# Casting v without DVE, loads held back by one-element writes, and longer planned DMA latencies in a fused attention and feed-forward kernel

## The chip, the cores and the metric

The kernel runs on one core of one Trainium2 chip. Its time is the device time of one execution in microseconds; "the time" of a kernel is the median of its runs. A profile is taken of one further execution.

The engines are named as the profile names them: PE (TensorE, matmuls), PEld (its weight loads, which overlap the matmuls), DVE (VectorE), ACT (ScalarE), POOL (GpSimd) and SP (SyncE, which only issues DMAs here). SPq and POOLq are the sequencers of SP and POOL.

## The reference

Attention with normalized q and k over 8 batches of 12 heads (448 positions, 64 wide), followed by a feed-forward layer of 3584 rows:

```python
def rmsnorm(x, g):
    rms = np.sqrt(np.mean(x * x, axis=-1, keepdims=True) + 1e-06)
    return x / rms * g
q_n, k_n = (rmsnorm(q, g_q), rmsnorm(k, g_k))
scores = scale * np.matmul(q_n, k_n.transpose(0, 1, 3, 2))
attn = np.exp(scores - np.max(scores, axis=-1, keepdims=True))
attn = attn / (np.sum(attn, axis=-1, keepdims=True) + 1e-09)
x = np.matmul(attn, v)          # heads side by side: (3584, 768)
h = x @ w_in                    # (3584, 2048)
g = h * np.clip(h + 3.0, 0.0, 6.0) / 6.0
out = g @ w_out                 # (3584, 768)
```

## The kernel before, in words

Heads are taken two at a time: 48 pairs, six to a batch. Each pair goes through these steps, whose lines are those that the profile shows:

- **Load.** k, q and v of a pair come in by DMA into slots of the staging tiles `qk_st` (k at index 0, q at index 1) and `v_st`, eight slots each (`NS`). From pair 4 on, the first 384 positions of two pairs come with one DMA (`load_main`, L325), and the last 64 of four pairs with one DMA for q (`load_rest`, L331) and two for k and for v (L333). All of these are issued on SP's queue. A load may overwrite its slot once the pair eight before has been read.
- **Norm.** Squares (`square`, L356 on POOL or DVE, L354 on ACT), sums over 64 (`sums`, L359, DVE), the reciprocal root (`rstd`, L365 and L366, ACT), and the product in bfloat16 (`normalize`, L369, POOL or DVE), which writes `qkn`. For the first eight pairs (`NFAST`) the squares and normalizations come in halves that several engines may take; later they are POOL's.
- **Transposes.** Eight PE transposes (L385) into PSUM, then copies to `qkT` (L397, L399, L336). From pair 20 on a DMA transpose on SP's queue (L390) takes their place.
- **Scores and weights.** Score matmuls (L408), the exponential on ACT (L418), and the weighted sum with v (`weigh`, L431), whose stationary operand is the exponentials and whose moving operand is `vaug`. `vaug` is v of the pair in bfloat16 with a column of ones, one of four buffers (`NV`); it is filled by `cast_v`, L336. So the cast for pair p waits until pair p - 4 has been weighed.
- **Division and x.** DVE divides (L439, L440); `xn` is transposed by PE and copied by DVE into `xT` (L450, L461), or from pair 18 on by a DMA transpose (L454).
- **Feed-forward.** Once six pairs of a batch are in `xT`, the first matrix (L464, `h_mm`), the gate on ACT and DVE (L470, L475), then the second matrix (L483, `y_mm`), the copy to `y_sb` (L336) and the store (L494, L496) on SP's queue. The weights come by DMAs on POOL's queue (L348), which cast to bfloat16 on the way.

The order of every engine's instructions is written by a planner in Python (`Plan`) when the program is built. It keeps a clock for each engine, a price for each operation on each engine that may do it (`ways`), and a model of the DMA queues: `ISSUE` is the time of an issue, `DEPART` the time until a transfer starts to flow, `LAND` the time from its end until the data may be used, and `size` the time for which it occupies the queue. At each step it begins, on each free engine, the ready operation with the least key. Engines are in-order: what the planner puts first runs first, and every instruction waits for what it really depends on, by semaphores. A dependency that only the planner is told of does not become a wait on the chip.

`slot_free` is such a list of dependencies for a load: the normalizations (for v the casts) of the pairs that were in the slots before, and from pair 8 on also the normalizations of the pair `LA` = 4 back. The first part is a true dependency on the tile. The second is only the planner's: the chip does not wait for it.

Of the kernel before, what the change touches and what calls it, by code (L numbers as in the profile page):

```python
# [44 lines left out]
class Plan:  # L45
# [1 line left out]

    HOP = 60
    PRICE, FIRST, UNTIL = {"POOL": 0.5, "ACT": 2.0, "DVE": 1.5}, {"POOL": 0.7, "ACT": 1.5, "DVE": 0.9}, 45e3
    ISSUE, DEPART, LAND, BULK, DEPTH = 620, 1000, 1100, 0.64, 8  # L50
    STEADY, SLACK, LATE = 60e3, 500, {"load": 3500, "turn": 2000}
    LAG = {"POOL": 45, "ACT": 105, "DVE": 85}
    UNITS = 4
# [9 lines left out]
    def add(self, key, ways, deps=(), lag=0, size=0, hold=False, want=None, cell=None):  # L63
        op = Op(key, ways, deps, lag, size, want, cell)
        op.left += hold
        op.subs = 0
        self.todo += 1
        if op.left == 0:
            self.known.append(op)
        return op  # L70
# [155 lines left out]
def kernel(  # L226
# [11 lines left out]
    nc = tc.nc  # L238
# [13 lines left out]
    NS = 8  # L252
# [19 lines left out]
    qk_st = const.tile([P, 2, NS, 2, 4, D], FP32, name="qk_st")  # L272
# [27 lines left out]
    plan = Plan(share=(1.3, 1.0, 0.45, 3.0, 0.4))  # L300
    add = plan.add
# [9 lines left out]
    def blocks(src):  # L311
        return src[:, 0:FULL, :].rearrange("h (p t) d -> p h (t d)", t=NT)

    def halves_of(src):
        return [src[h::2, FULL:S, :].rearrange("h p d -> p h d") for h in range(2)]

    def stage(a, p, n):

        r = slice(p % NS, p % NS + n)
        return heads((k, q, v)[a], p, n), v_st[:, r] if a == 2 else qk_st[:, a, r]  # L320

    def load_main(eng, a, p, n):
        src, st = stage(a, p, n)
        dst = st.rearrange("p r h t d -> p (r h) t d")
        eng.dma_start(out=dst[:, :, 0:NT, :].rearrange("p h t d -> p h (t d)"), in_=blocks(src))  # L325

    def load_rest(eng, a, p, n, half):
        src, st = stage(a, p, n)
        if a == 1:
            dst = st.rearrange("p r h t d -> p (r h) t d")[lo, :, NT, :]  # L330
            eng.dma_start(out=dst, in_=src[:, FULL:S, :].rearrange("h p d -> p h d"))  # L331
        else:
            eng.dma_start(out=st[(lo, hi)[half], :, half, NT, :], in_=halves_of(src)[half])  # L333

    def copy(eng, out, in_):
        (eng.copy if eng is nc.scalar else eng.tensor_copy)(out=out, in_=in_)  # L336
# [38 lines left out]
    def cast_v(eng, p):  # L375
        copy(
            eng, out=vaug[p % NV][:, :, :, 0:D].rearrange("p t h d -> p h t d"),
            in_=v_st[:, p % NS],
        )
# [140 lines left out]
    def load_g(eng):  # L520
        for dst, src in ((gq_t, g_q), (gk_t, g_k)):
            eng.dma_start(out=dst[lo, :], in_=src.rearrange("(p o) -> p o", o=1))
# [7 lines left out]
    V, G, A_ = nc.vector, nc.gpsimd, nc.scalar  # L530
# [4 lines left out]
    def at(xs, i):  # L535
        return xs[i] if 0 <= i < len(xs) else None
# [5 lines left out]
    nrm, vc, tr, pq, pk, wgh, div, xo, px = ([] for _ in range(9))  # L542
# [78 lines left out]
    W_AFTER, LA, VL = 2, 4, 1.2  # L621
# [16 lines left out]
    kb = 780  # L638
    landed, squares, norms = ({}, {}, {}), [], {}

    def slot_free(a, p, n, ahead):

        old = [x for i in range(p, p + n) for x in ([vc[i - NS]] if a == 2 else norms[i - NS]) if i >= NS] \
            if p >= NS else []
        return old + norms.get(p - ahead, []) * (p >= 8)

    def load(a, p, main, rest, rank, aq=nc.sync, qq="SP"):
        if main:
            op = plan.dma((p + rank, a), 1, main * 580, lambda: load_main(aq, a, p, main), slot_free(a, p, main, LA), queue=qq)
            for i in range(p, p + main):  # L650
                landed[a].setdefault(i, []).append(op)
        if rest:
            for half in range(1 if a == 1 else 2):
                op = plan.dma((p + rank, a + 0.1), 1, rest * (200 if a == 1 else 100),
                              lambda half=half: load_rest(aq, a, p, rest, half), slot_free(a, p, rest, LA), queue=qq)
                for i in range(p, p + rest):
                    landed[a].setdefault(i, []).append(op)
        return op

    lg = mg = None  # L660
    for p in range(NPAIR):
        if p == 0:
            lg = plan.dma((-3, 0), 2, 10, lambda: load_g(nc.gpsimd), queue="POOL", issue=900)
            for a, aq, qq in ((0, nc.sync, "SP"), (1, nc.scalar, "ACT")):
                load(a, 0, 1, 1, 0, aq, qq)
            load(0, 1, 1, 0, 0)
            load(1, 1, 1, 0, 0, nc.scalar, "ACT")
            load(0, 1, 0, 3, 0.2)
            load(1, 1, 0, 3, 0.2)
            add((1, 1.5), [("ACT", 1300, lambda: nc.scalar.preload_act_table_set("natural_log_exp_and_others"))])  # L670
            mg = add((-1, 0), [("DVE", 300, make_g)], [lg])
            load(0, 2, 2, 0, 0)
            load(1, 2, 2, 0, 0)
            load(2, 0, 2, 4, V0)
            lv = load(2, 2, 2, 0, V2)
            for w in w_ops:
                lv.next.append(w)
        elif p in REST_OF or p in MAIN_OF:
            for a in range(3):
                load(a, p, MAIN_OF.get(p, 0), REST_OF.get(p, 0), VL if a == 2 else 0)  # L680

# [28 lines left out]
        for a in range(2):  # L710
            ways = [("POOL", 1000, lambda p=p, a=a: normalize(G, p, a)), ("DVE", 1200, lambda p=p, a=a: normalize(V, p, a))]
            norms[p].append(add((p - 2, 4), ways[:2 if p < NFAST else 1], [s2[a], at(tr, p - NQ)]))
        vc.append(add((p, 5), [("DVE", 700, lambda p=p: cast_v(V, p)),
                               ("POOL", 575, lambda p=p: cast_v(G, p)),
                               ("ACT", 530, lambda p=p: cast_v(A_, p))],
                      [*landed[2][p], at(clo, p), at(clv, p // 2), weighed.get(p - NV)]))

        old = scored.get(p - NK, [])
# [4 lines left out]
        else:  # L723
            cell = {}
# [101 lines left out]
```

## Time and profile before

| what | us |
|---|---|
| time, median of 3 runs (lowest to highest) | 446.86 (446.25 to 447.33) |
| the profiled execution's own time | 448.29 |
| its span | 446.5 |
| DVE busy | 243.0 |
| ACT busy | 259.6 |
| POOL busy | 211.1 |
| DMA queue of SP, share of 16 engines' span | 51.0% |
| DMA queue of POOL, share | 10.2% |

The span is from the first to the last instruction of the profiled execution, and its own time has what lies around it. In the lists of groups a row has the line, the engine, the operation, the tile written and read, shapes and the number of instructions; then the busy time and the mean of one. In the timeline a row has its start, its length, and in brackets how long the engine sat idle before it and what ended that. In a table of stretches the busy times of PE, PEld, DVE, ACT and POOL follow the length, each with the number of instructions, and then the granted clock of PE as a share of full speed, the DMA share and GB/s. Rows for a tile or a line give the least, median and greatest duration in nanoseconds.

### The profile page before, as it was taken

To read this page: it belongs to the slowest core of one execution; us is meant where nothing else is said; L and a number is where in the kernel's file an instruction comes from. 1 tells how busy PE (TensorE), PEld (TensorE's weight loads), DVE (VectorE), ACT (ScalarE), POOL (GpSimd) and SP (SyncE) were. 2 spreads that over 40 slices of the span, in tenths; PEclk is the share of its full clock that TensorE was granted. 3 is DMA by queue.
4 is the path that set the end of the run, shared out by engine and by line. 5 is a ranking of instruction groups with operands and counts; after the bars stand their busy time and mean duration, and the time that the engine had idled before them with its cause. 6 is when DMAs were issued, how large, how long until landed. Compare 5 with 4: busy or idle time off the path is not lost.

```text
span 446.5 us, 9002 instructions
## 1 busy us (share of the span) xinstructions
PE 415.3 (93%) x3576; PEld 235.9 (53%) x3576; DVE 243.0 (54%) x421; ACT 259.6 (58%) x478; POOL 211.1 (47%) x204
## 2 busy tenths in 40 slices
PE   0878499999999999999999999999999999999995
PEld 0445265545655555555455655555556555555563
DVE  6899698866864466445546355333435243343321
ACT  3979278987567687777767577676652032132100
POOL 5999569988886676667637554401100000000000
PEclk9989599999999999999999999999999999999999
DMA  7999909999838999886885775243212301100021
GB/s 198 261 255 245 245 0 201 241 258 209 193 94 189 213 193 218 155 215 151 187 202 139 182 164 136 47 95 84 72 24 60 84 1 52 56 37 35 37 72 71
DMA packets 118011, 62.21 MB, mean 139 GB/s; under 512 B 67280, under 2 KB 114384, under 8 KB 117968
## 3 DMA queue, kind: packets, MB, share of 16 engines
q1 hardware_dynamic: 106784, 54.90, 51.0%
q0 software_dynamic: 10496, 6.29, 10.2%
q8 instruction: 28, 0.46, 0.5%
q10 hardware_dynamic: 688, 0.43, 0.3%
q14 instruction: 15, 0.12, 0.1%
HBM read 45.61 MB, written 11.01 MB: 127 GB/s over the span
## 4 chain that ended last, share of the span: by engine, by line
PE 69%; POOL 10%; DVE 7%; DMA 7%; issue 3%; SPq 2%; ACT 1%; POOLq 0%; DVEq 0%; ACTq 0%
PE ps L483 25%; PE ps L464 23%; PE av L431 6%; PE sc L408 6%; PE sc L483 5%; POOL qkn L369 5%; DMA qk_st<-in_q_dram 5%; POOL sq L356 4%; DVE ssq L359 2%; DVE vaug L336 2%; PE sc L464 2%; DMA qkT<-qkn 1%; DVE gT L475 1%; SPq L333 1%; DMA gk_t<-in_g_k_dram 1%
## 5 line engine op out<-in xcount | busy, mean ns | idle before, releaser
L464 PE MATMUL ps<-xT,w_in_sb 128*128 128x448 bf16 x732 | 169.2, 355 | 7.9 <-DVE xT L461 5.9
L418 ACT ACTIVATE eD<-sc 128x896 bf16<-128x896 f32 x144 | 127.3, 915 | 31.7 <-PE sc L408 25.6
L483 PE MATMUL ps<-w_out_sb,gT 128*128 128x384 bf16 x752 | 141.4, 326 | 1.2 <-DVE gT L475 1.1
L470 ACT ACTIVATE t_sb<-ps 128x448 f32<-128x448 f32 x122 | 66.3, 543 | 91.1 <-PE ps L464 87.9
L475 DVE SCALAR_TENSOR_TENSOR gT<-t_sb,ps 128x448 bf16<-128x448 f32 x122 | 75.4, 618 | 72.3 <-ACT t_sb L470 72.0
L483 PEld LDWEIGHTS <-gT 128*128 128x128 bf16 x896 | 82.0, 98 | 60.9 <-issue 12.9
L369 POOL TENSOR_TENSOR qkn<-qk_st,rstd 128x512 bf16<-128x512 f32 x90 | 93.6, 1059 | 26.9 <-ACT rstd L366 16.8
L464 PEld LDWEIGHTS <-w_in_sb 128*128 128x128 bf16 x768 | 68.7, 98 | 63.9 <-issue 18.4
L356 POOL TENSOR_TENSOR sq<-qk_st 128x1024 f32<-128x1024 f32 (+1 forms) x49 | 85.8, 1761 | 7.2 <-DMA qk_st<-in_q_dram 5.7
L431 PEld LDWEIGHTS <-eD 128*128 128x128 bf16 x1152 | 53.6, 99 | 22.6 <-issue 4.5
L359 DVE TENSOR_REDUCE ssq<-sq 128x16 f32<-128x1024 f32 (+1 forms) x50 | 58.3, 1169 | 12.0 <-POOL sq L356 11.2
L408 PE MATMUL sc<-qkT 64*128 64x448 bf16 (+1 forms) x336 | 60.4, 364 | 3.2 <-ACT qkT L336 1.2
L336 DVE COPY y_sb<-ps 128x384 f32<-128x384 f32 x42 | 23.4, 557 | 72.2 <-PE ps L483 72.2
L431 PE MATMUL av<-vaug,eD 128*128 128x65 bf16 x1152 | 59.9, 195 | 0.0
L336 POOL CAST vaug<-v_st 128x512 bf16<-128x512 f32 x34 | 20.8, 618 | 77.6 <-PE av L431 77.6
L440 DVE TENSOR_TENSOR xn<-av,rden 128x512 bf16<-128x512 f32 x48 | 33.2, 692 | 1.7
L418 ACT ACTIVATE eR<-sc 128x448 bf16<-128x448 f32 x48 | 25.9, 539 | 11.4 <-PE sc L408 11.2
L408 PEld LDWEIGHTS <-qkT 64*128 64x128 bf16 (+1 forms) x336 | 14.4, 95 | 30.2 <-issue 24.8
L483 PE MATMUL sc<-w_out_sb,gT 128*128 128x384 bf16 x144 | 25.5, 326 | 0.0
L385 PE MATMUL ps<-identity,qkn 128*128 128x128 bf16 x120 | 11.0, 237 | 13.7 <-POOL qkn L369 11.5
L385 PEld LDWEIGHTS <-qkn 128*128 128x128 bf16 x160 | 11.1, 106 | 17.0 <-POOL qkn L369 11.9
L431 PE MATMUL av<-vaug,eR 128*128 128x130 bf16 x192 | 19.2, 224 | 0.0
(51 smaller groups left out, 178.2 us busy)
## 6 DMA issues: line engine op xcount, KB each, us to landing
v_st<-in_v_dram SPq DMA_DIRECT2D x24, 384.0 KB, 5.8
out_dram<-y_sb SPq DMA_DIRECT2D x24, 384.0 KB, 2.8
qk_st<-in_k_dram SPq DMA_DIRECT2D x23, 384.0 KB, 6.0
qk_st<-in_q_dram SPq DMA_DIRECT2D x23, 384.0 KB, 5.2
w_in_sb<-in_moe_w_in_dram POOLq DMA_DIRECT2D x8, 384.0 KB, 7.3
w_out_sb<-in_moe_w_out_dram POOLq DMA_DIRECT2D x4, 768.0 KB, 11.0
v_st<-in_v_dram SPq DMA_DIRECT2D x24, 64.0 KB, 4.9
out_dram<-y_sb SPq DMA_DIRECT2D x8, 192.0 KB, 2.9
```

The costliest lines, as they stand in the source:

```text
L336: (eng.copy if eng is nc.scalar else eng.tensor_copy)(out=out, in_=in_)
L356: eng.tensor_tensor(out=sq, in0=x, in1=x, op=A_MULT)
L359: nc.vector.tensor_reduce(out=ssq_r[p % NR][:, a].rearrange("p a s -> p (a s)"), in_=sq_r[m % 2][:, a].rearrange("p a s d -> p (a s) d"), ...
L369: eng.tensor_tensor(out=qkn_r[p % NQ][:, a].rearrange("p t h d -> p h t d"), in0=qk_st[:, a, p % NS], in1=rstd_r[p % NR][:, a].rearrange(" ...
L408: nc.tensor.matmul(out=bank(u, h)[:, 0:S], lhsT=qkT[rows, 0, i * P:(i + 1) * P], rhs=qkT[rows, 1, 0:S], start=True, stop=True,)
L418: nc.scalar.activation(out=e[..., 0:S], in_=src[..., 0:S], func=EXP, bias=0.0, scale=1.0)
L431: nc.tensor.matmul(out=out, lhsT=e_tile(p, i, h)[:, c0:c0 + P], rhs=rhs, start=first and j % 2 == 0 and h == 0, stop=last, skip_group_chec ...
L440: nc.vector.tensor_tensor(out=xn_r[p % NQ][:].rearrange("p n (h d) -> p n h d", h=2), in0=av4[:, :, :, 0:D], in1=rden[:].unsqueeze(3).to_b ...
L464: nc.tensor.matmul(out=bank(m)[:, 0:S], lhsT=w_in_sb[:, kt, f * P:(f + 1) * P], rhs=xT[:, kt, b % NX, x_slot(b)], start=(kt == 0), stop=(k ...
L470: nc.scalar.activation(out=t[:], in_=bank(m)[:, 0:S], func=RELU, bias=0.5, scale=1.0 / 6.0,)
L475: nc.vector.scalar_tensor_tensor(out=gT[:, f, (b % 2) * S:(b % 2 + 1) * S], in0=t[:], scalar=1.0, in1=bank(m)[:, 0:S], op0=A_MIN, op1=A_MULT,)
L483: nc.tensor.matmul(out=bank(m)[:, 0:n], lhsT=gT[:, f, c0:c0 + P], rhs=w_out_sb[:, f, c:c + n], start=(f == 0), stop=(f == NFT - 1),)
```

## The change

Three things change, all in the program's text for the planner, with one new kind of instruction:

1. `cast_v` may be done by POOL or ACT, no longer by DVE.
2. For each even pair from 8 to 46, POOL writes one element of zero into k's slot of that pair (`hold`), placed in the plan after the normalizations of the pairs four and eight back. The loads of that pair depend on it in the plan; the load of k that covers the element also does on the chip, since both write the same place. `slot_free` no longer has the planner's own dependency.
3. The planner's numbers: `ISSUE` 630 (620), `DEPART` 1300 (1000), `LAND` 1400 (1100), and the size of the rest loads 150 and 75 for each pair (200 and 100).

```diff
-    ISSUE, DEPART, LAND, BULK, DEPTH = 620, 1000, 1100, 0.64, 8
+    ISSUE, DEPART, LAND, BULK, DEPTH = 630, 1300, 1400, 0.64, 8
...
-    def slot_free(a, p, n, ahead):
+    def slot_free(a, p, n):
 
         old = [x for i in range(p, p + n) for x in ([vc[i - NS]] if a == 2 else norms[i - NS]) if i >= NS] \
             if p >= NS else []
-        return old + norms.get(p - ahead, []) * (p >= 8)
+        return old
+
+    held = {}
+
+    def hold(p):
+
+        cell = qk_st[0:1, 0, p % NS, 0, 0, 0:1]
+        held[p] = [add((-5, p), [("POOL", 80, lambda: nc.gpsimd.memset(cell, 0.0))], norms[p - LA] + norms[p - NS])]
 
     def load(a, p, main, rest, rank, aq=nc.sync, qq="SP"):
         if main:
-            op = plan.dma((p + rank, a), 1, main * 580, lambda: load_main(aq, a, p, main), slot_free(a, p, main, LA), queue=qq)
+            op = plan.dma((p + rank, a), 1, main * 580, lambda: load_main(aq, a, p, main), slot_free(a, p, main) + held.get(p, []), queue=qq)
...
-                op = plan.dma((p + rank, a + 0.1), 1, rest * (200 if a == 1 else 100),
-                              lambda half=half: load_rest(aq, a, p, rest, half), slot_free(a, p, rest, LA), queue=qq)
+                op = plan.dma((p + rank, a + 0.1), 1, rest * (150 if a == 1 else 75),
+                              lambda half=half: load_rest(aq, a, p, rest, half), slot_free(a, p, rest) + held.get(p, []), queue=qq)
...
         elif p in REST_OF or p in MAIN_OF:
+            if p >= NS:
+                hold(p)
             for a in range(3):
                 load(a, p, MAIN_OF.get(p, 0), REST_OF.get(p, 0), VL if a == 2 else 0)
...
-        vc.append(add((p, 5), [("DVE", 700, lambda p=p: cast_v(V, p)),
-                               ("POOL", 575, lambda p=p: cast_v(G, p)),
+        vc.append(add((p, 5), [("POOL", 575, lambda p=p: cast_v(G, p)),
                                ("ACT", 530, lambda p=p: cast_v(A_, p))],
                       [*landed[2][p], at(clo, p), at(clv, p // 2), weighed.get(p - NV)]))
```

The built program issues, on POOL, 35 casts of v (34 before), 89 normalizations (90), 7 half squares (9) and the 20 one-element writes; on ACT 13 casts (11), 8 half squares (6) and 11 copies of y (5); on DVE no cast (3), 7 normalizations (6), 45 copies of y (51). SP issues the same DMAs, in the same order until its 69th.

## The prediction

> **What bounds the kernel now.** I read the page's busy times first, then the table of stretches, then PE's waits, then the timeline around the longest of them.
>
> ```profile
> span 446.5 us, 9002 instructions
> PE 415.3 (93%) x3576; PEld 235.9 (53%) x3576; DVE 243.0 (54%) x421; ACT 259.6 (58%) x478; POOL 211.1 (47%) x204
> PEclk9989599999999999999999999999999999999999
> ```
>
> TensorE is busy for 415.3 of 446.5 us, so the end moves only with PE's 31.2 idle us or with the clock at which it works. The clock line (tenths of full speed, 40 slices of 11.2 us) has one deep dip, in the fifth slice (44.7 to 55.8 us), and a slight one in the third. PE's waits, in the view that names who let it go:
>
> ```profile
> PE ps L385 <- POOL qkn L369: 11.5, 3, 10.6
> PE ps L464 <- DVE xT L461: 5.9, 1, 5.9
> PE ps L385 <- DVE qkn L369: 2.1, 2, 1.8
> PE ps L464 <- DVE gT L475: 1.5, 2, 0.9
> ```
>
> The columns are total, times and longest. Of the 11.5, 10.6 us are the start, before any data. The next is one wait of 5.9 us, for a copy of xT by DVE. Everything else is below 2 us a piece. The timeline shows what DVE was doing:
>
> ```profile
> 42.62 4.04 POOL L369 TENSOR_TENSOR qkn<-qk_st,rstd 128x512 bf16<-128x512 f32 x4
> 43.78 6.86 DVE L336 CAST vaug<-v_st 128x512 bf16<-128x512 f32 x1
> 46.62 3.73 POOL L356 TENSOR_TENSOR sq<-qk_st 128x1024 f32<-128x1024 f32 x2
> 50.31 0.86 POOL L348 DMA_DIRECT2D w_in_sb<-in_moe_w_in_dram  x1
> 50.56 0.38 DVE L461 COPY xT<-ps 128x448 bf16<-128x448 bf16 x1
> 50.87 0.54 DVE L336 CAST vaug<-v_st 128x512 bf16<-128x512 f32 x1
> 51.00 2.40 PE L464 MATMUL ps<-xT,w_in_sb 128*128 128x448 bf16 x6 [5.86 <-DVE xT L461]
> ```
>
> A cast of v took 6.86 us on DVE; the next one of the same shape took 0.54. The long one ends at 50.64, 0.29 us after POOL's unbroken run of four normalizations and two squares ends (46.62 + 3.73 = 50.35). Six POOL instructions in a row kept DVE's cast out. Behind the cast stood the copy of xT, and behind that PE. The price goes on after the wait:
>
> ```profile
> 45.00:51.00 6.00, 0.14 (x4) 0.02 (x1) 6.00 (x3) 0.63 (x1) 6.00 (x5) 0.62 1.22 272
> 51.00:57.40 6.40, 6.40 (x39) 3.40 (x39) 2.72 (x6) 1.95 (x3) 0.17 (x1) 0.55 0.80 160
> 57.40:64.00 6.60, 6.60 (x81) 4.19 (x78) 6.00 (x12) 5.25 (x12) 4.37 (x4) 1.00 0.00 0
> 60.00:110.00 50.00, 47.81 (x523) 27.58 (x523) 39.49 (x72) 40.82 (x82) 46.80 (x40) 1.00 1.00 197
> 110.00:344.00 234.00, 232.31 (x2098) 129.93 (x2095) 118.52 (x197) 161.55 (x286) 119.44 (x108) 1.00 0.65 145
> 344.00:442.00 98.00, 98.00 (x577) 55.67 (x575) 34.40 (x59) 18.46 (x34) 0.00 (x0) 1.00 0.14 47
> ```
>
> Each row is a stretch, its length, busy time of PE, PEld, DVE, ACT and POOL, then the granted clock. From 51.0 to 57.4 PE works without a gap at a granted clock of 0.55; from 57.4 on it has 1.00. After 60 us PE idles 2.19 us (50 - 47.81) up to 110, 1.69 us up to 344, and not at all from there to 442. The head is where time can be won. POOL, with 46.80 of 50 us from 60 to 110, is the engine that could take PE's place there.
>
> **The change part by part.** Durations come from the profiled execution, which took 448.29 us around its span of 446.5; the runs' median is 446.86, 1.43 us less. I work out a difference against the profiled execution and apply it to the median.
>
> *v never cast by DVE.* All three casts leave DVE. The long one's wait goes: 5.86 us of PE. Its cold stretch goes too: 6.40 us at 0.55 cost 0.45 x 6.40 = 2.88 us. Sum **-8.74 us**. What is late next? POOL was busy right through the stall, and its normalizations for pairs 8 and 9 (42.62 to 46.66) were done when PE would have needed them. After 50.31 POOL had nothing but a wait, because DVE's sums had been held up as well:
>
> ```profile
> 59.63 2.03 POOL L369 TENSOR_TENSOR qkn<-qk_st,rstd 128x512 bf16<-128x512 f32 x2 [8.45 <-ACT rstd L366]
> L336 POOL CAST vaug<-v_st x34: 608/618/623, 14.4 to 323.1; 128x512 bf16<-128x512 f32 x34
> L336 ACT CAST vaug<-v_st x11: 612/627/636, 22.3 to 220.8; 128x512 bf16<-128x512 f32 x11
> L369 POOL TENSOR_TENSOR qkn<-qk_st,rstd x90: 1031/1042/1517, 9.5 to 288.3; 128x512 bf16<-128x512 f32 x90
> L369 DVE TENSOR_TENSOR qkn<-qk_st,rstd x6: 693/1479/3030, 12.0 to 36.5; 128x512 bf16<-128x512 f32 x6
> ```
>
> So POOL's chain can move forward by those 8.45 us together with PE; I see no second wait right behind the first. In the changed program's order ACT casts 13 (was 11) and POOL 35 (was 34). POOL also has two half squares and one normalization fewer, which go to ACT and DVE. POOL in the head: 0.62 - 3 x 1.04 = -2.5 us. ACT: 2 x 0.63 for the casts and 2 x 0.62 for the squares, beside 42% idle. DVE: one more normalization, 0.69 us if it runs at once and 3.03 if it is kept out like the worst here. I take 0 and keep -2.5 and +2.3 (3.03 - 0.69) for the range; without its idle time ACT would cost PE 2.5.
>
> *The one-element writes.* Twenty on POOL, for pairs 8, 10, up to 46. The nearest rows are POOL's own fills at the start:
>
> ```profile
> 0.24 0.10 POOL L810 MEMSET const-float32-0.0<- 128x1 f32 x1 [0.24 <-issue]
> 3.12 1.25 POOL L518 MEMSET eD<- 128x128 bf16 x8
> ```
>
> Between 0.10 and 1.25/8 = 0.16 us each, that is 2.0 to 3.2 us of POOL in all; six lie between 60 and 110, about 0.6 to 1.0 us. POOL's lighter head covers that: 0, and +1.0 if POOL sets the pace. The writes wait for nothing new on POOL: the normalization of the pair four back is ahead of them in POOL's own order.
>
> *What the writes hold back.* This is the cost I can see least. The load of k for pair p waits on SP for the write into its slot, and q, v, later loads, stores and DMA transposes queue behind it. Before, the load ran far ahead:
>
> ```profile
> 18.96 1.01 SPq L325 DMA_DIRECT2D qk_st<-in_k_dram  x1
> 20.40 1.49 SPq L333 DMA_DIRECT2D qk_st<-in_k_dram  x2
> 21.95 0.60 SPq L325 DMA_DIRECT2D qk_st<-in_q_dram  x1
> 22.64 0.93 SPq L331 DMA_DIRECT2D qk_st<-in_q_dram  x1
> 38.04 3.74 POOL L356 TENSOR_TENSOR sq<-qk_st 128x1024 f32<-128x1024 f32 x2
> qk_st<-in_q_dram SPq DMA_DIRECT2D x11, 128.0 KB, 4.8
> DMA to landing us min/median/max: 2.7/4.6/13.2
> ```
>
> k of pair 8 was issued at 18.96 and squared at 38.04, a lead of 19 us. In the new order POOL has, between the write for pair 8 and that square, one weight issue (0.88), three normalizations (3.12), three casts (1.85) and the write for pair 10 (0.10): 5.95 us of work. The load needs five issues of about 0.6 us (k, its two rests, q, its rest) and 4.8 us to land, 7.8 us. So POOL would stand 1.85 us at that square. Bounds: 0, if the casts' waits for PE (each needs the v buffer of the pair four back) already fill that time; and 13.1, if one hold meets the longest landing of the row above, 13.2 us (3.0 + 13.2 - 5.95 = 10.2) and leaves PE cold behind it (2.88). I take **+1.0**, half of the 1.85 at the median landing: PE has feed-forward matmuls to fill with, and lost only 2.19 us from 60 to 110 though POOL was 94% busy. Behind a load that waits on SP stand the stores and, from pair 20 on, the DMA transposes that PE's scores need; by then a pair takes PE longer than the 7.8 us.
>
> *Longer latencies in the plan.* Nothing new is issued; the planner sets what depends on a load later (departure and landing 2.7 us instead of 2.1). Its best is the 3.88 us that PE still idles between 60 and 344; its worst, from the same rows, as much again. The loads' landing of 4.8 us is nearer to the new numbers than to the old, so I take **-0.5**.
>
> Sum: -8.74 + 1.0 - 0.5 = -8.24. Profiled execution 448.29 - 8.24 = 440.0; median 446.86 - 8.24 = **438.6 us**. With no lateness from the holds and all 3.88 us of waits gone it would be 446.86 - 8.74 - 3.88 = 434.2; with two holds late by their full 1.85 and nothing from the plan, 446.86 - 8.74 + 3.7 = 441.8. That is this case's own range.
>
> **The rivals.** *Another instruction is kept out instead.* DVE's normalizations suffer the same: the row above has 693 ns at best and 3030 at worst. One of them cost PE time:
>
> ```profile
> 28.91 0.40 PE L385 MATMUL ps<-identity,qkn 128*128 128x128 bf16 x4 [1.77 <-DVE qkn L369]
> 28.90:32.60 3.70, 3.39 (x29) 2.30 (x30) 3.67 (x7) 2.73 (x4) 3.70 (x4) 0.57 1.20 262
> ```
>
> That is 1.77 + 0.43 x 3.70 = 3.4 us. The change leaves seven normalizations and one square on DVE (six and one before), and POOL's new order has, from the normalization of pair 5 to the square of pair 8, 3 x 1.04 + 3 x 0.62 + 1.89 = 6.9 us with no weight issue in it. For it: a run as long as the one that kept the cast out. Against: POOL's casts wait there for PE, which breaks the run. Price between 3.4 and all 8.74: 442.0 to 447.3; I take 443.5, nearer to the price that was seen. The Trainium skill, "SBUF — State Buffer", section "Who interferes with whom", says that a DVE instruction with two SBUF inputs also contends with a GpSimd instruction that reads SBUF, not only the copies in the two-port modes; by that rule the change leaves eight contenders of ten. The trace agrees (3030 against 693 ns).
>
> ```profile
> 10.00:50.00 40.00, 28.17 (x319) 17.59 (x320) 37.55 (x47) 31.62 (x63) 38.37 (x36) 0.91 1.19 257
> ```
>
> *The holds make POOL late: slower.* From 10 to 50 us the DMA share is 1.19, no free time, so the first holds (pairs 8 and 10) may meet landings near 13.2 us rather than 4.8. One such wait and the cold clock after it cost 13.1: 446.86 - 8.74 - 0.5 + 13.1 = 450.7. Six holds up to pair 18, each late by the median's 1.85 us with nothing made up, come to 11.1 and 448.7. It decides once the holds cost PE 9.2 us together. For it: a lead of 19 us cut to 6, and POOL without slack. Against: loads were held before too, by the slots of their rests (pair 12's until 38.10, pair 16's until 67.29), and the waits of PE above name no load.
>
> ```profile
> 38.10 1.56 SPq L333 DMA_DIRECT2D qk_st<-in_k_dram  x2
> 67.29 1.27 SPq L333 DMA_DIRECT2D qk_st<-in_k_dram  x2
> POOL sq L356 <- DMA qk_st<-in_q_dram: 5.7, 4, 3.0
> ```
>
> *The new order clears more than the one stall.* Also the wait at 28.91 goes (3.4) and half of the later 3.88: 438.6 - 3.4 - 1.4 = 433.8. For it: the lighter POOL head. Against: the order of PE hardly differs, and DVE has more normalizations.
>
> *The writes do not hold.* They touch k's slot alone; q and v are held only by SP's order. If loads run ahead as before, the 1.0 falls away: 437.6, inside my range.
>
> **How the numbers follow.** Forecast 0.52, kept-out instruction 0.24, late holds 0.12, cleared order 0.12. About 0.2% (0.9 us) is what a measurement of this kernel tells from no change. Faster: 0.50 of the first, 0.18 of the second, all 0.12 of the last, 0.80. Same: 0.05, mostly the second case's dear end. Slower: 0.15, the 0.12 of late holds and the worst of the others. The range takes in the second case up to no gain and most of the fourth: 432.5 to 446.9; the late holds and the best of the fourth are left out.
>
> **What would show it.** Right: no cast of v on DVE, no PE wait over 3 us after the start, a clock of 1.00 between 44 and 58 us, PE busy about 412 (415.3 - 2.88), POOL's 8.45 us wait gone. The holds show as POOL squares waiting for qk_st (5.7 us in all before): more than 10 us means the late holds. A kept-out instruction shows as a DVE normalization or square of over 3 us and a new dip of the clock. I am wrong if PE idles elsewhere by more than 5 us, or if POOL waits for loads from pair 8 on.

## The result, and the profile after

| | before | after |
|---|---|---|
| time, median (lowest to highest), 6 runs each on the same chip | 447.57 (446.25 to 448.02) | 441.12 (439.20 to 442.29) |
| the profiled execution's own time | 448.29 | 439.20 |
| its span | 446.5 | 437.4 |

The ratio is 0.9857, 95% interval 0.9825 to 0.9889: 6.45 us faster. From the page of the changed kernel, its span, its busy times and its clock line:

```profile
span 437.4 us, 9008 instructions
...
PE 412.1 (94%) x3576; PEld 234.6 (54%) x3576; DVE 230.3 (53%) x411; ACT 265.9 (61%) x490; POOL 209.2 (48%) x222
...
PEclk9989999999999999999999999999999999999999
```

The deep dip in the fifth slice is gone; the slight one in the third stays. PE is busy for 3.2 us less, with as many matmuls: most of that is the 2.88 us of the cold stretch, which it now does at full clock instead of 0.55. PE's longest waits (total, times, longest):

```profile
PE ps L385 <- POOL qkn L369: 9.7, 2, 9.5
PE sc L408 <- ACT eD L418: 2.9, 6, 0.8
PE ps L464 <- DVE gT L475: 2.2, 2, 1.3
PE sc L408 <- ACT qkT L336: 1.6, 1, 1.6
```

The 5.9 us behind xT is not in the list, nor is the 1.8 us behind a normalization of DVE. Where the 9.1 us of the span came from is read from a table of stretches for PE alone (length, PE busy with its instructions, granted clock, DMA share, GB/s). Before:

```profile
0.00:20.00 20.00, 7.80 (x64) 1.00 0.92 222
20.00:40.00 20.00, 15.90 (x210) 0.91 1.21 266
40.00:60.00 20.00, 13.47 (x117) 0.74 0.89 185
```

After:

```profile
0.00:20.00 20.00, 8.09 (x72) 1.00 0.92 230
20.00:40.00 20.00, 16.29 (x206) 0.91 1.05 221
40.00:60.00 20.00, 18.48 (x214) 1.00 0.93 167
60.00:110.00 50.00, 46.01 (x481) 1.00 1.13 221
110.00:344.00 234.00, 233.98 (x2097) 1.00 0.66 147
```

PE's idle time is length less busy time. From 40 to 60 it fell from 6.53 to 1.52 us, and there the clock rose from 0.74 to 1.00. From 60 to 110 it rose, from 2.19 (the row quoted before) to 3.99; from 110 to 344 it fell from 1.69 to 0.02. The first 40 us gave 0.68, the tail 0.4. In all 5.9 us of idle time and 3.2 of busy time: 9.1.

Where the 1.8 us from 60 to 110 went shows in the timeline of POOL, SP, DVE and PE around pair 12 (start, length, in brackets the idle time before and what ended it):

```profile
47.51 0.09 POOL L652 MEMSET qk_st<- 1x1 f32 x1
...
47.63 0.37 SPq L325 DMA_DIRECT2D qk_st<-in_k_dram  x1
...
49.74 0.55 SPq L325 DMA_DIRECT2D qk_st<-in_q_dram  x1
...
53.40 0.62 POOL L336 CAST vaug<-v_st 128x512 bf16<-128x512 f32 x1
...
57.90 1.89 POOL L356 TENSOR_TENSOR sq<-qk_st 128x1024 f32<-128x1024 f32 x1 [3.88 <-DVE gT L475]
...
59.82 1.22 DVE L359 TENSOR_REDUCE ssq<-sq 128x16 f32<-128x1024 f32 x1 [2.13 <-POOL sq L356]
...
60.96 0.61 DVE L475 SCALAR_TENSOR_TENSOR gT<-t_sb,ps 128x448 bf16<-128x448 f32 x1
...
61.62 0.54 PE L464 MATMUL ps<-xT,w_in_sb 128*128 128x448 bf16 x2 [1.34 <-DVE gT L475]
```

The write into pair 12's slot starts at 47.51, and k's load is issued 0.03 us after it ends (31.83 before the change); q follows at 49.74. POOL is free at 54.0 and stands 3.88 us at the square of that pair. DVE waits for the square, its next gate waits behind the sums, and PE waits 1.34 us for that gate. The row names a gate of DVE as what ended POOL's wait; the experiment that follows with the same order shows that it was the load.

### The profile page after: what moved, and what is told of

Its sections match the earlier page's. It is cut to its first block, busy times and chain, and to the rows that moved or that the text cites. A ratio compares the mean times of both kernels' runs of the same rounds, so it can differ in the third digit from the quotient of the medians.

```text
span 437.4 us, 9008 instructions
## 1 busy us (share of the span) xinstructions
PE 412.1 (94%) x3576; PEld 234.6 (54%) x3576; DVE 230.3 (53%) x411; ACT 265.9 (61%) x490; POOL 209.2 (48%) x222
## 4 chain that ended last, share of the span: by engine, by line
PE 84%; DVE 5%; DMA 3%; POOL 3%; issue 2%; ACT 1%; SPq 1%; POOLq 0%; DVEq 0%
PE ps L483 30%; PE ps L464 29%; PE av L431 9%; PE sc L408 8%; PE sc L483 4%; DMA qk_st<-in_q_dram 2%; DVE ssq L359 2%; PE sc L464 2%; POOL sq L356 2%; PE ps L385 1%; DVE qkn L369 1%; DVE qkT L399 1%; DMA qk_st<-in_k_dram 1%; POOL qkn L369 1%; DVE gT L475 0%
## 5 line engine op out<-in xcount | busy, mean ns | idle before, releaser
L464 PE MATMUL ps<-xT,w_in_sb 128*128 128x448 bf16 x726 | 167.1, 353 | 3.1 <-DVE gT L475 2.2
L483 PE MATMUL ps<-w_out_sb,gT 128*128 128x384 bf16 x784 | 145.8, 326 | 0.0
L369 POOL TENSOR_TENSOR qkn<-qk_st,rstd 128x512 bf16<-128x512 f32 x89 | 91.6, 1048 | 18.0 <-DMA qkT<-qkn 8.7
L356 POOL TENSOR_TENSOR sq<-qk_st 128x1024 f32<-128x1024 f32 (+1 forms) x47 | 83.4, 1787 | 7.3 <-DVE gT L475 3.9
L359 DVE TENSOR_REDUCE ssq<-sq 128x16 f32<-128x1024 f32 (+1 forms) x50 | 58.2, 1168 | 10.3 <-POOL sq L356 10.0
L336 POOL CAST vaug<-v_st 128x512 bf16<-128x512 f32 x35 | 22.5, 648 | 79.5 <-PE av L431 72.4
L431 PE MATMUL av<-vaug,eD 128*128 128x65 bf16 x1152 | 58.2, 194 | 0.0
L336 DVE COPY y_sb<-ps 128x384 f32<-128x384 f32 x38 | 21.2, 557 | 57.3 <-PE ps L483 57.1
L439 DVE RECIPROCAL rden<-av 128x8 f32<-128x8 f32 x48 | 9.8, 204 | 30.1 <-PE av L431 30.0
L397 ACT ACTIVATE qkT<-qkT,gprime 128x448 bf16<-128x448 bf16 x28 | 18.7, 668 | 1.2 <-DMA qkT<-qkn 1.2
L483 PE MATMUL sc<-w_out_sb,gT 128*128 128x384 bf16 x112 | 19.3, 326 | 0.0
```

What stands on the lines that cost most here:

```text
L356: eng.tensor_tensor(out=sq, in0=x, in1=x, op=A_MULT)
L359: nc.vector.tensor_reduce(out=ssq_r[p % NR][:, a].rearrange("p a s -> p (a s)"), in_=sq_r[m % 2][:, a].rearrange("p a s d -> p (a s) d"), ...
L369: eng.tensor_tensor(out=qkn_r[p % NQ][:, a].rearrange("p t h d -> p h t d"), in0=qk_st[:, a, p % NS], in1=rstd_r[p % NR][:, a].rearrange(" ...
L431: nc.tensor.matmul(out=out, lhsT=e_tile(p, i, h)[:, c0:c0 + P], rhs=rhs, start=first and j % 2 == 0 and h == 0, stop=last, skip_group_chec ...
L464: nc.tensor.matmul(out=bank(m)[:, 0:S], lhsT=w_in_sb[:, kt, f * P:(f + 1) * P], rhs=xT[:, kt, b % NX, x_slot(b)], start=(kt == 0), stop=(k ...
L483: nc.tensor.matmul(out=bank(m)[:, 0:n], lhsT=gT[:, f, c0:c0 + P], rhs=w_out_sb[:, f, c:c + n], start=(f == 0), stop=(f == NFT - 1),)
```

## The experiments

The theory (A): DVE's cast was kept out by POOL's unbroken run because of the form of the instruction, and behind it PE lost first time and then clock; taking the cast off DVE is the whole gain, and the holds give a part of it back. The rivals: the gain comes from the new order; or the holds and latencies bring it.

### The cast alone, in the order of before

Three kernels keep the order of before word for word and change only what the three casts of DVE are. The first emits them on ACT, at the places which the plan has for them on DVE:

```diff
-        vc.append(add((p, 5), [("DVE", 700, lambda p=p: cast_v(V, p)),
+        vc.append(add((p, 5), [("DVE", 700, lambda p=p: cast_v(A_, p)),
```

> The kernel before with its whole order kept; only its three DVE casts of v are given to ACT, at the same place of the plan (ACT needs 0.63 us for one). Theory (the cast kept out by POOL is the whole gain): PE's wait of 5.86 us at xT and the cold stretch of 2.88 us go, so the time falls by 8.7 us, to about 0.980 of before (7.5 to 9.5 us), without holds and without new latencies. Rival (the gain came from the reordered plan or the holds): the stall at 45 to 51 us goes, but PE waits for something else there, and the time falls by less than 4 us (ratio above 0.991).

Measured: 439.83 us (439.13 to 440.46), ratio 0.9855 (0.9817 to 0.9893), 7.1 us below the kernel before on the same chip (446.96). Its PE has no wait behind xT, and from 40 to 60 us it idles 1.27 us, 5.3 less than before:

```profile
40.00:60.00 20.00, 18.73 (x217) 1.00 0.90 187
```

So the gain needs no new order, no holds and no latencies.

The second leaves them on DVE, as a sum over one element, which has one input:

```diff
-        vc.append(add((p, 5), [("DVE", 700, lambda p=p: cast_v(V, p)),
+        vc.append(add((p, 5), [("DVE", 700, lambda p=p: V.tensor_reduce(
+            out=vaug[p % NV][:, :, :, 0:D].rearrange("p t h d -> p h t d"),
+            in_=v_st[:, p % NS].unsqueeze(4), axis=mybir.AxisListType.X, op=A_ADD)),
```

> The kernel before with its whole order kept; its three DVE casts stay on DVE, at the same place, but are written as a sum over one element, a DVE instruction with one SBUF input and, by theory, outside the copies' fast modes. Theory (what keeps the cast out is a port of SBUF that only copies and two-input instructions share with POOL): each takes about 0.55 to 0.7 us, none is stretched, PE's wait at xT goes and the time falls by 7.5 to 9.5 us (ratio about 0.980). Rival (any DVE work that reads SBUF is held up while POOL runs without a break, or the data of v came late): one still takes over 5 us and the time stays within 1.5 us of before.

Measured: 439.03 us (438.90 to 439.16), ratio 0.9836 (0.9790 to 0.9882). The tile's row (least, median and greatest ns):

```profile
L713 DVE TENSOR_REDUCE vaug<-v_st x3: 677/678/678, 34.8 to 44.2; 128x512 bf16<-128x512 f32 x3
```

And its timeline, of POOL and DVE:

```profile
42.15 4.04 POOL L369 TENSOR_TENSOR qkn<-qk_st,rstd 128x512 bf16<-128x512 f32 x4
...
43.31 0.68 DVE L713 TENSOR_REDUCE vaug<-v_st 128x512 bf16<-128x512 f32 x1
...
46.16 3.73 POOL L356 TENSOR_TENSOR sq<-qk_st 128x1024 f32<-128x1024 f32 x2
...
50.73 2.05 POOL L369 TENSOR_TENSOR qkn<-qk_st,rstd 128x512 bf16<-128x512 f32 x2
```

The same cast, on the same engine, at the same place, beside the same run of POOL: 0.68 us instead of 6.86. From 40 to 60 us PE idles 1.53 us, 5.0 less than before. And POOL goes on at 50.73 rather than standing 8.45 us: that wait was a result of the stall.

The third gives DVE's cast two inputs, as the maximum of v and v:

```diff
-        vc.append(add((p, 5), [("DVE", 700, lambda p=p: cast_v(V, p)),
+        vc.append(add((p, 5), [("DVE", 700, lambda p=p: V.tensor_tensor(
+            out=vaug[p % NV][:, :, :, 0:D].rearrange("p t h d -> p h t d"),
+            in0=v_st[:, p % NS], in1=v_st[:, p % NS], op=mybir.AluOpType.max)),
```

> The kernel before with its whole order kept; the three DVE casts are written as the maximum of v with itself, so an instruction with two SBUF inputs. Theory A (two-input instructions are kept out as copies are, by the whole run of POOL): one takes over 6 us and the time stays within 1.5 us of before. Theory B (they get in between two POOL instructions, as the normalizations at 17.45 and 29.07 seem to): at most about 1.9 + 0.7 us each, PE's wait below 2 us, and the time falls by 5 to 8.5 us.

Measured: 447.83 us (446.87 to 448.28), ratio 1.0029 (1.0000 to 1.0058). The tile's row, the timeline, and PE's longest wait after the start:

```profile
L713 DVE TENSOR_TENSOR vaug<-v_st x3: 678/1025/7127, 35.2 to 51.1; 128x512 bf16<-128x512 f32 x3
```

```profile
43.71 7.13 DVE L713 TENSOR_TENSOR vaug<-v_st 128x512 bf16<-128x512 f32 x1
...
46.55 3.73 POOL L356 TENSOR_TENSOR sq<-qk_st 128x1024 f32<-128x1024 f32 x2
...
50.23 0.86 POOL L348 DMA_DIRECT2D w_in_sb<-in_moe_w_in_dram  x1
```

```profile
PE ps L464 <- DVE xT L461: 6.1, 1, 6.1
```

When nothing is in its way it takes 0.68 us as well, but here 7.13, until POOL's run ends at 50.28 and half a microsecond beyond, and the whole loss is back. So it is the form that decides, and an instruction with two inputs in SBUF is kept out as long as a copy. The Trainium skill says in "SBUF — State Buffer", section "Who interferes with whom", that a sum by `tensor_reduce` never contends with GpSimd on trn2 and one with two SBUF inputs does; 678 ns and 7127 ns agree.

### The cast alone, replanned

```diff
-        vc.append(add((p, 5), [("DVE", 700, lambda p=p: cast_v(V, p)),
-                               ("POOL", 575, lambda p=p: cast_v(G, p)),
+        vc.append(add((p, 5), [("POOL", 575, lambda p=p: cast_v(G, p)),
```

> The kernel before with only the first part of the change: DVE may not cast v, the planner makes its order anew. Theory (this part is the gain): 7 to 9 us faster, ratio 0.980 to 0.985, as with the order kept (439.83). Rival (a new order brings its own waits): more than 2.5 us from that value, either way, with the difference in PE's idle time before 110 us.

Measured: 438.91 us (437.94 to 439.47), ratio 0.9830 (0.9792 to 0.9868), span 437.4. The row of its table of stretches:

```profile
40.00:60.00 20.00, 19.34 (x231) 1.00 0.96 195
```

PE's idle time there is 0.66 us, 5.87 less than before; the two kernels in the order of before have 5.3 and 5.0 less. The span is that of the changed kernel to the tenth, so in the profiled executions the holds and latencies together are worth nothing; in the medians (441.12, and 441.03 for the changed kernel once more on this chip) they cost 2.1 us.

### The holds, in the order of after

The order stays that of the changed kernel, the 20 writes too, but they go to a tile of their own, so no load waits for them:

```diff
-        cell = qk_st[0:1, 0, p % NS, 0, 0, 0:1]
+        cell = spare[0:1, 0:1]
```

> The changed kernel with its whole order kept; the twenty one-element writes go to a spare tile, so that no load waits for them on the chip. Theory (the holds cost: POOL's square of pair 12 stood 3.88 us at 57.90 for a load issued only at 47.63): that wait goes, PE's idle time from 60 to 70 us falls from 2.8 to about 1, and the time is 1 to 3 us under the changed kernel's (ratio to before 0.979 to 0.984). Rival (the holds help, by keeping loads out of the weights' way): the time is 1 us or more above the changed kernel's (ratio 0.988 or more), with PE waiting for the gate or the weights between 45 and 70 us. Within 1 us: the holds do not matter.

Measured: 438.40 us (437.64 to 439.22), ratio 0.9824 (0.9782 to 0.9867), span 436.0: 2.7 us below the changed kernel in the medians, 1.4 in the profiled executions. Its timeline, and the row of the stretch from 60 to 110:

```profile
29.88 0.79 SPq L325 DMA_DIRECT2D qk_st<-in_k_dram  x1
...
53.96 1.89 POOL L356 TENSOR_TENSOR sq<-qk_st 128x1024 f32<-128x1024 f32 x1
...
59.56 0.62 DVE L475 SCALAR_TENSOR_TENSOR gT<-t_sb,ps 128x448 bf16<-128x448 f32 x1 [0.75 <-ACT t_sb L470]
```

```profile
60.00:110.00 50.00, 47.34 (x489) 1.00 1.10 220
```

k of pair 12 leaves at 29.88, its square starts at 53.96 without a wait, and the gate behind it at 59.56 instead of 60.96. PE works 1.33 us more from 60 to 110; from 40 to 60 and from 110 to 344 PE's busy time agrees within 0.01 us. So the square waited for the held load, and 1.33 of the 1.4 us is the 1.34 us wait of PE above. The writes are issued in both, so between the two profiled executions the difference is that wait; the 2.7 us of the medians is more than this trace shows.

The changed kernel once more, beside the kernel with the cast alone:

> The changed kernel once more, beside the others of this call. Theory (the holds cost 2 to 3 us): 440 to 442 us, 2 to 3 us above the kernel with its writes in a spare tile (438.4). Rival (the difference between the two was the chip or the clock's phase): 438 to 439.5 us.

Measured: 441.03 us (439.88 to 443.30), ratio 0.9885 (0.9842 to 0.9928). From POOL's waits, and from its timeline:

```profile
POOL sq L356 <- DMA qk_st<-in_q_dram: 7.3, 6, 2.8
```

```profile
37.57 1.89 POOL L356 TENSOR_TENSOR sq<-qk_st 128x1024 f32<-128x1024 f32 x1 [1.06 <-DMA qk_st<-in_q_dram]
...
58.56 1.89 POOL L356 TENSOR_TENSOR sq<-qk_st 128x1024 f32<-128x1024 f32 x1 [2.83 <-DMA qk_st<-in_q_dram]
```

Here the profile itself names the load, at pair 8 (1.06) and pair 12 (2.83). PE's rows of this execution:

```profile
40.00:60.00 20.00, 17.50 (x184) 0.91 0.96 179
60.00:110.00 50.00, 47.05 (x490) 1.00 1.12 218
```

From 40 to 110 us PE idles 5.45 us (5.51 in the first profile, 4.17 with the spare tile). But only 0.29 us of it stands behind the gate that cost 1.34 there; the rest of the difference lies ahead of 60 us. So about the same price, 1.3 us, comes again in another place, though this trace doesn't tie all of it to held loads.

Without the writes, the distance known to the planner alone, all else as in the changed kernel:

```diff
-        held[p] = [add((-5, p), [("POOL", 80, lambda: nc.gpsimd.memset(cell, 0.0))], norms[p - LA] + norms[p - NS])]
+        held[p] = norms[p - LA]
```

> The changed kernel without the writes, the planner's own dependency on the pair four back put back in their place: parts one and three. Theory (part two costs): 437 to 440 us, as the kernel with the writes in a spare tile, no POOL square of pair 8 to 16 waiting over 2 us for a load. Rival (holds pay once the plan is made anew): 441 us or more.

Measured: 437.22 us (436.65 to 440.33), ratio 0.9809 (0.9766 to 0.9851). It is the lowest median of all, ahead of the changed kernel by 3.8 us, and no POOL square waits over 1.1 us in its trace.

### Earlier holds

```diff
-    W_AFTER, LA, VL = 2, 4, 1.2
+    W_AFTER, LA, VL = 2, 6, 1.2
```

> The changed kernel with LA = 6 instead of 4: the planner may place each one-element write after the normalizations of the pair six back (and eight back, as before), so the loads of a pair may leave two pairs earlier; everything else is planned as in the changed kernel. Theory A (the holds cost time because the load leaves too late: without them 437.2, with them 441.0): the writes move forward, POOL's squares wait less than 2 us for qk_st, and the median falls to 437 to 439.5. Rival B (the 20 writes and the true dependency that they add cost by themselves, or the load has to wait for the slot's last reader anyway): 440.5 to 442.

Measured: 440.09 us (439.17 to 440.55), ratio 0.9869 (0.9823 to 0.9916), between the two ranges. The loads did leave earlier: k of pair 12 at 34.27 instead of 47.63. POOL's square of pair 8 (32.32) has no wait and that of pair 10 waits 0.17 us (timeline, then the row of the stretch):

```profile
34.27 0.37 SPq L325 DMA_DIRECT2D qk_st<-in_k_dram  x1
...
38.28 1.90 POOL L356 TENSOR_TENSOR sq<-qk_st 128x1024 f32<-128x1024 f32 x1 [0.17 <-DMA qk_st<-in_q_dram]
```

```profile
60.00:110.00 50.00, 46.24 (x468) 1.00 1.09 217
```

No later square waits for a load before 110 us, yet PE idles 3.76 us from 60 to 110, nearly as much as in the changed kernel (3.99). Its longest waits of this stretch are for a copy of qkT (0.93) and a gate (0.92): the new plan has its own. So late loads are what the holds cost in one order; taking the lateness away by replanning doesn't give it back by itself.

### No holds, and the cast on DVE in the free form

```diff
+        vc.append(add((p, 5), [("DVE", 700, lambda p=p: V.tensor_reduce(...)),
-        vc.append(add((p, 5), [("POOL", 575, lambda p=p: cast_v(G, p)),
+                               ("POOL", 575, lambda p=p: cast_v(G, p)),
```

(on the kernel without the writes)

> The changed kernel without the one-element writes (the planner alone keeps the distance), and DVE may cast v again, but as a tensor_reduce over one element, which ran in 678 ns beside POOL. Theory A (only the form of the instruction kept DVE's cast out, not the engine): no cast on DVE over 1 us, no stall of PE behind xT, and 436 to 438.5, the same as without DVE's casts (437.2). If a third engine for the casts relieves POOL's waits it may come to 435 to 436. Rival B (a replanned order puts DVE's casts ahead of work that PE needs): 438.5 to 441.

Measured: 439.98 us (438.31 to 441.12), ratio 0.9865 (0.9815 to 0.9914): where B put it. The planner gave DVE two casts, each of 677 ns, and PE has no wait over 0.4 us behind xT. The tile's row:

```profile
L722 DVE TENSOR_REDUCE vaug<-v_st x2: 677/677/677, 38.8 to 43.2; 128x512 bf16<-128x512 f32 x2
```

That a third engine for the casts wins anything is not shown. With the earlier holds this gives a measure of what a new order alone does: four plans without a long cast on DVE and without a late load in the head came to 437.2, 438.9, 440.0 and 440.1 (no writes; the cast alone; no writes with the reduce form; earlier holds). A difference of under 3 us between two replanned kernels can't be put down to the edit.

### Holds with the old latencies

```diff
-    ISSUE, DEPART, LAND, BULK, DEPTH = 630, 1300, 1400, 0.64, 8
+    ISSUE, DEPART, LAND, BULK, DEPTH = 620, 1000, 1100, 0.64, 8
```

(and the sizes of the rest loads as before)

> The changed kernel with the planner's old latencies, so parts one and two. Theory (the holds make loads late, and the longer latencies let the plan allow for it): POOL's squares wait longer for loads than in the changed kernel, PE idles 1 to 4 us more before 110 us, 441 to 445 us. Rival (the latencies change nothing that matters): within 1.5 us of the changed kernel.

Measured: 446.86 us (442.15 to 448.04), ratio 0.9999 (0.9969 to 1.0028): in the median the cast's whole gain is gone, which neither expectation had. The profiled execution was the 442.15 one, with a span of 440.3. From PE's waits, and two rows of its table of stretches:

```profile
PE ps L385 <- DVE qkn L369: 2.7, 3, 1.8
```

```profile
60.00:110.00 50.00, 47.28 (x481) 1.00 1.16 227
110.00:344.00 234.00, 231.82 (x2075) 1.00 0.62 142
```

PE idles 2.18 us from 110 to 344, where the changed kernel has 0.02, and waits again for a normalization of DVE, as with the cast alone. The span is 2.2 us over that of the changed kernel on the same chip (438.1); the other 4.7 us of the median execution are not in this trace. Nor does it show the late loads of the theory: from 20 to 110 us POOL's squares wait 0.2 us for loads, where the changed kernel on the same chip has 3.9, and up to 110 us PE idles 1.1 us less than there, not 1 to 4 more. The same kernel once more:

> The same kernel as old_latency (no cast on DVE, with the holds, the old planned latencies) once more, for a profile of one of its more frequent executions: ten of its twelve took 446.3 to 448.0, the profiled one 442.15 with PE waiting nowhere over 2 us after the start. Theory A (in the frequent executions one late load makes PE wait long enough for the clock to fall): a PE wait of 2 us or more after 30 us, behind a POOL square or normalization that waited for qk_st, and a second stretch with a granted clock of 0.83 or less in a 10 us window. Rival B (no single wait: many small ones): PE's waits from 30 to 344 us add up to 4 us more than in the profile of old_latency, none over 1.5 us, and the clock dips once, as there. If the profile falls on the faster kind again, it stays open.

Measured: 446.39 us (442.17 to 447.64), ratio 0.9981 (0.9938 to 1.0023), the profile again on a short execution (443.46, no PE wait over 1.8 us after the start). 17 of the 22 executions took 446.1 to 448.0, five 442.2 to 443.5. Their mean granted clocks, 0.986 to 0.996 against 0.994 to 0.996, differ by 0.003 in the median, at most some 1.2 us of PE's 413. What the rest of the 4 to 5 us between the two kinds is stays open.

## Why the prediction was right

The forecast was 438.6 with a range of its own of 434.2 to 441.8; the median was 441.12. For the profiled execution it was 440.0, measured 439.2. That this agrees within 0.8 us is in part luck: 0.68 us in the first 40 us and 1.67 from 110 to 344, of which the sum had only the 0.5 of the latencies, made up for the 1.8 us lost from 60 to 110.

*-5.86, the wait behind the cast.* Right in cause, and nearly in size: 5.3 and 5.0 us of PE's idle time from 40 to 60 in the order of before, 5.87 with the cast alone, whose order is new; 7.1 to 8.3 us in the medians for this step and the next together (the cast on ACT, in the reduce form, and replanned), 8.74 predicted. The two-input control brought the loss back.

*-2.88, the cold stretch.* Right: PE busy 412.1 where "about 412" was written, clock 1.00 from 44 to 58 us (the row of that stretch after):

```profile
44.00:58.00 14.00, 13.24 (x157) 8.51 (x158) 10.04 (x20) 9.65 (x20) 10.04 (x13) 1.00 0.92 169
```

*What is late next: nothing.* Right: from 40 to 60 PE idles 1.52 us, and POOL's wait of 8.45 us is gone (the longest that the trace after puts down to `rstd` is 2.3 us).

*The casts on ACT and POOL, the writes: 0.* Nothing speaks against it. The median cast takes 621 ns on POOL and 619 on ACT. A write takes 0.09 us; what the twenty cost as instructions was not tried by itself.

*The holds, +1.0.* The mechanism was right, a late load at a POOL square, and in the profiled execution the size too: 1.4. The place was not. I put it at pair 8, with 1.85 us of lateness; there POOL stood 2.21 us at a cast for PE, which I had named as the bound that makes the cost nothing, and the square had no wait in this execution. It was pair 12. POOL had 6.4 us of work between write and square (47.60 to 54.02), and 10.3 us passed until the square could begin, where I had 7.8: the issues went nearly as I had them (q at 49.74, 2.1 us after the write), but from there it took 8.2 us and not 4.8. "I am wrong if POOL waits for loads from pair 8 on" was too strict: POOL did wait, and PE lost a third of it. In the medians the term is mis-sized: 2.7 us in the same order, not 1.0.

*The longer latencies, -0.5.* Not settled as a number. Without holds, 1.7 us in the medians (438.91 to 437.22), less than what a new order alone does. With holds 5.8 us (446.86 to 441.03). Read the other way, on one chip, the holds cost 8.0 us under the old latencies (438.91 to 446.86) and 3.8 under the new (437.22 to 441.03): the two parts aren't independent terms, as the sum had them. Why the holds cost so much under the old latencies stays open; the two traced executions, both short ones, show no late load behind it.

*From the profile to the median.* This is the step that missed: "I work out a difference against the profiled execution and apply it to the median". The profiled executions differ by 9.09 us, the medians by 6.45. The profiled execution of before lay 0.7 us above its median of six, that of after 1.9 us below its own. Of the 2.5 us by which the median lies above the forecast, 1.8 is the gain that falls short (8.24 - 6.45); the other 0.7 is that the median of before is 447.57 here and was 446.86 in the three runs shown. The twelve runs of the changed kernel fall in two halves, 439.2 to 440.2 with a mean granted clock of 0.996 and 441.9 to 443.3 with 0.9915 (means of six). The clock can account for at most 0.0045 x 412 = 1.9 us of the 2.5 between their means: the mean is taken over the whole span, PE's waits included, and two of the slower six (441.9 at 0.995, 442.1 at 0.994) have nearly the clock of the others. Without the holds in the same order the six runs end at 439.22, so the slower half comes with the holds. What makes it slower is not shown: both profiles of the changed kernel fell on the faster half.

*The rivals.* Another instruction kept out: no. DVE's seven normalizations took at most 1778 ns (3030 before) and its one square 2196, below the 3 us that I had set, and the dip in the third slice was there before. Late holds, slower: no for this change; with the old latencies the held kernel gains nothing in the median (446.86), but no trace puts that down to a late load. The cleared order: in part. The wait of 1.77 us at 28.91 went, and 1.67 us from 110 to 344; 1.8 us from 60 to 110 was paid for it. The writes do not hold: no; k's load leaves 0.03 us after its write.

## What to carry to other kernels

When one engine's instruction shows ten times its usual duration, look at what runs without a break beside it, and try the same work in a form that does not share what they contend for: here a sum over one element gave the whole gain on the same engine and in the same order. A true dependency that keeps a load at the planned distance makes the work behind it late when the load takes longer than the plan's distance allows: here 10.3 us passed where POOL had 6.4 us of work to fill them. Leaving the order to the queue was 2.7 us better. To price one part of a planned kernel, hold the order fixed and change the part: replanned variants without a long cast or a late load in the head lay 3 us apart.

## What the runs showed that I had not expected

A DVE instruction kept out by POOL waits not for one POOL instruction but for what is left of the run: 6.86 us (copy) and 7.13 us (two inputs), begun in the second of six POOL instructions of 1.0 to 1.9 us each, until POOL issued a DMA.

And the kernel before is in effect two kernels. Of its 17 runs beside the kernels in the order of before, four took 442.6 to 443.4 us at a mean granted clock of 0.996, thirteen 446.5 to 448.1 at 0.983 to 0.987; of all 51 runs beside the experiments, 42 were of the long kind. The profiled execution is a long one. Its clock fell to half at 46.46 and rose at 56.70, and those 10.24 us lower the mean by 0.0115, about the difference between the two kinds:

```profile
43.04:46.46 3.42, 1.65 (x14) 1.00 1.11 190
46.46:51.00 4.54, 0.00 (x1) 0.50 1.21 290
51.00:56.70 5.70, 5.70 (x36) 0.50 0.90 179
56.70:60.11 3.41, 3.41 (x32) 1.00 0.00 0
```

But 4.54 of the 10.24 us lie in PE's wait, where a slow clock costs nothing. Half of the other 5.70 is the cold stretch of 2.9 us, and the two kinds lie 4.3 us apart (means of the 17 runs). So a short run seems to be one in which the clock doesn't fall, and 1.4 us of its lead have another cause; no short run was traced.

The Trainium skill, "TensorE: Matmul & The Clock Gate", section "What's actually happening", says that PE's clock gate watches free-running windows of 3.41 us and closes, to half clock, after an idle one. The trace agrees with the windows, as 10.24 us are three times 3.41, but not with the idle one: the clock fell 1.3 us after PE's last matmul ended (45.14), and in the 3.42 us before it fell PE was busy for 1.65, 48%. The changed kernel shows the same at its slight dip, with no wait of PE over 0.8 us near it:

```profile
21.19:24.60 3.41, 2.10 (x24) 1.00 1.20 235
24.60:28.02 3.42, 3.31 (x28) 0.50 0.43 58
58.74:62.15 3.41, 2.07 (x13) 1.00 1.14 302
```

After 62% busy the clock fell for one window (24.60 to 28.02); after 61% behind the wait of 1.34 us (58.74 to 62.15) it stayed. So waits shorter than a window are enough here, and where the limit lies is not settled.
